# Preparing the first four attention units in another way: powers in PSUM, scaling on VectorE, the bonus by TensorE

## The chip, the cores and the metric

One core of one Trainium2 chip runs the whole kernel. The metric is the device time of one execution in microseconds; the number that stands for a kernel is the median of its runs.

## What is computed

Three stages follow each other. The first is a linear attention with a decaying state (4 sequences, 8 heads, 768 steps, head size 48), the other two are feed-forward networks over its 3072 output rows:

```
cur   = u * k_t (outer) v_t
y_t   = r_t . (state + cur)            # u is the bonus of the present step
state = w * state + k_t (outer) v_t    # w is the decay, one number per head and channel
h = max(x @ w1, x @ w2, x @ w3);  x = h @ w_out               # 384 -> 768 -> 384
g = x @ w_gate;  out = (silu(g) * (x @ w_val)) @ w_out2       # 384 -> 1536 -> 384
```

Everything is float32. A matmul of the networks is made of three at a faster type: each operand is split into a high part and a low part (`xhi`, `xlo` for inputs, two halves of `w_a`, `w_b`, `w_c` for weights), and the low times low product is left out.

## The kernel before

The 768 steps are six blocks of 128. With 4 sequences that makes 24 units; unit n is block n // 4, sequence n % 4. Blocks, not units, go through the networks: one block has 512 rows.

**A unit.** `load_unit` (L284) brings `qk` (r and k with channels down the partitions, 448 KB) and `nat` (k, v and r with time down the partitions, 576 KB). `prep_scores` (L299) multiplies r and k by a table `P` of powers of the decay, `scores` (L326) forms the 128x128 products per head in two PSUM banks. `prep_bonus` (L303) makes k * r * u on GpSimd, `bonus` (L312) sums it over a head's channels on VectorE into `a`, `fill` (L317) writes a diagonal matrix of it into `am` on ScalarE, eight instructions a unit, and `select` (L334) copies the scores below the diagonal over it on VectorE. `apply` (L341) multiplies `am` with v into the bank `y`; from unit 4 on it adds the state's part. `evacuate` (L364) copies `y` into the block's input `xr`. `prep_keys` (L308), `outer` (L371) and `update` (L389) keep the state.

**Weights.** They arrive in raw form and are rebuilt on the chip: a job k is half of a weight tile, fetched by SyncE (`fetch`), scaled on ScalarE (L225), put together by three VectorE instructions (L258, L259, L265), cast to the high half on ScalarE (`put_hi`, L270), and subtracted to give the low half (`put_lo`, L273, GpSimd or VectorE). There are three raw buffers, so fetch k waits for the last step of job k - 3.

**The first four units** (block 0) are prepared before any network work can begin. Before them VectorE builds `P` by doubling. When their rows are copied out, a branch follows (`branch`, L605): if a decay lies outside a range, a slow general loop recomputes everything. On these inputs it is not taken. Only after the branch are block 0's rows split into `xhi` (ScalarE, L410) and `xlo` (L414), and TensorE begins with m(0,0,0): the key m(i,f,j) is block i, output tile f of six, matrix j of three, nine matmuls of 128x512. Units 4 to 7 are prepared between block 0's groups, o(0,c) is the second product of the first network.

**The order** is written by a planner, `Plan` (L88). Each step names the engines that can do it with an estimated cost, and the steps it needs; TensorE's order is fixed by a list, and the others are filled in by estimated start times. Steps that share a read port between VectorE and GpSimd are listed in `SHARED`. Where the plan expects TensorE to stand still, `idle` inserts spare matmuls (`warm`). DMAs rotate over eight semaphores, so SyncE can issue a transfer only when the one eight places earlier has landed.

At the start SyncE also writes three blocks of zeros (768 KB each) to memory, `y_far` (L529): the inputs that the branch's general loop would have filled for blocks 3 to 5.

Of the kernel before, what the change touches and what calls it, by code (L numbers as in the profile page):

```python
# [88 lines left out]
class Plan:  # L89
# [9 lines left out]
    SHARED = ("top", "rest", "lo", "xlo", "ylo", "scaled", "bonus", "choose")  # L99
# [8 lines left out]
    def run(self, idle, hop=0.1):  # L108
# [32 lines left out]
        while ready:  # L141
# [4 lines left out]
            for k, options in ready.items():  # L146
                for e, t in options:
                    start, cost = max(t, free[e]), steps[k][0][e]
                    if e == "pool" or e == "dve" and k[0] in self.SHARED and (k[0], k[1] > 3) != ("scaled", True):
# [3 lines left out]
                    weight = rest[k] if k not in self.behind else rest[head] - self.behind[k]  # L153
                    rank = (start + shy - self.LOOK * weight, start + cost)
                    if best is None or rank < best[0]:
                        best = rank, k, e, start, cost
# [6 lines left out]
            if e == "pool" or e == "dve" and k[0] in self.SHARED and (k[0], k[1] > 3) != ("scaled", True):  # L163
# [10 lines left out]
def rwkv_moe(ctx: ExitStack, tc: tile.TileContext, qk, nat, kn, vn, rn, wcol, wh, uh, wup1, wout1, wup2, out):  # L174
# [106 lines left out]

    def load_unit(n):
        kvr = nat[n].rearrange("p (q h d) -> p q h d", q=3, h=H)
        if n in (2, 3):  # L284
            a = h_tile([112, 2, NPAIR, T], f"qk_{n}")
            c = h_tile([128, 2, H, D], f"kv_{n}")
            c = (c[:, 0], c[:, 1], r23[:, n - 2])
            nc.sync.dma_start(out=a, in_=qk[n].rearrange("p (q j t) -> p q j t", q=2, j=NPAIR))
            for x in range(3):
                nc.sync.dma_start(out=c[x], in_=kvr[:, x])  # L290
        else:
            a = atp.tile([112, 2, NPAIR, T], F32, tag="qk", name=f"qk_{n}")
            c = atp.tile([128, 3, H, D], F32, tag="nat", name=f"nat_{n}")
            nc.sync.dma_start(out=a, in_=qk[n].rearrange("p (q j t) -> p q j t", q=2, j=NPAIR))
            nc.sync.dma_start(out=c, in_=kvr)
            c = (c[:, 0], c[:, 1], c[:, 2])
        inp[n] = (a, c)

    def prep_scores(n, q, eng):  # L299
        a = inp[n][0][:, q]  # L300
        eng.tensor_tensor(out=a, in0=a, in1=late["P"] if n >= B else P[0:112], op=ALU.mult)
# [10 lines left out]
    def bonus(n):  # L312
# [590 lines left out]
```

## Time and profile before

| | us |
|---|---|
| runs | 860.22, 860.72, 862.56 (median 860.72) |
| profiled execution: its own time | 865.69 |
| profiled execution: span from first to last instruction | 864.0 |
| TensorE busy | 847.5 (98% of the span) |
| VectorE busy | 362.9 (42%) |
| ScalarE busy | 292.7 (34%) |
| GpSimd busy | 210.7 (24%) |
| mean granted TensorE clock | 0.993 |

Busy shares are averages over a start in which TensorE waits and a long rest in which it does not. In a timeline row, the idle time before an instruction and what ended it stand in brackets. A group's mean length mixes instructions that ran undisturbed with such that waited inside.

### The profile page before, as it was taken

To read this page: it belongs to the slowest core of one execution; us is meant where nothing else is said; L and a number is where in the kernel's file an instruction comes from. 1 tells how busy PE (TensorE), PEld (TensorE's weight loads), DVE (VectorE), ACT (ScalarE), POOL (GpSimd) and SP (SyncE) were. 2 spreads that over 40 slices of the span, in tenths; PEclk is the share of its full clock that TensorE was granted. 3 is DMA by queue.
4 is the path that set the end of the run, shared out by engine and by line. 5 is a ranking of instruction groups with operands and counts; after the bars stand their busy time and mean duration, and the time that the engine had idled before them with its cause. 6 is when DMAs were issued, how large, how long until landed. Compare 5 with 4: busy or idle time off the path is not lost.

```text
span 864.0 us, 11768 instructions
## 1 busy us (share of the span) xinstructions
PE 847.5 (98%) x4794; PEld 697.1 (81%) x4794; DVE 362.9 (42%) x545; ACT 292.7 (34%) x592; POOL 210.7 (24%) x188
## 2 busy tenths in 40 slices
PE   8889999999999999999999999999999999999998
PEld 7578678888888887888888888888888888888886
DVE  5578966627637735224377122222222222122221
ACT  5456553424434433213344221221122122113111
POOL 6756752514713702101224200010010010001000
PEclk9899999999999999999999999999999999999999
DMA  9567534445445632431132100010000000001001
GB/s 271 207 186 221 172 105 152 141 143 178 140 145 176 195 113 78 174 109 55 55 110 82 37 1 1 0 37 1 1 36 1 1 1 37 1 1 37 0 1 37
DMA packets 21720, 74.31 MB, mean 86 GB/s; under 512 B 2496, under 2 KB 3392, under 8 KB 20896
## 3 DMA queue, kind: packets, MB, share of 16 engines
q1 hardware_dynamic: 21664, 73.54, 26.2%
q8 instruction: 38, 0.62, 0.3%
q14 instruction: 18, 0.15, 0.1%
HBM read 58.39 MB, written 14.16 MB: 84 GB/s over the span
## 4 chain that ended last, share of the span: by engine, by line
PE 88%; DMA 3%; POOL 3%; DVE 2%; issue 2%; ACT 1%; SPq 1%; POOLq 0%; ACTq 0%; DVEq 0%
PE g L420 11%; PE g L421 11%; PE g L419 11%; PE m L419 8%; PE m L420 7%; PE m L421 7%; PE oo L420 6%; PE oo L421 6%; PE oo L419 6%; PE o L421 3%; PE o L419 3%; PE o L420 3%; PE s L332 2%; PE y L361 2%; PE y L352 2%
## 5 line engine op out<-in xcount | busy, mean ns | idle before, releaser
L419 PE MATMUL g<-xhi,w_c 128*128 128x512 f32 x432 | 168.0, 389 | 0.0
L420 PE MATMUL g<-xlo,w_c 128*128 128x512 f32 x432 | 168.0, 389 | 0.0
L421 PE MATMUL g<-xhi,w_c 128*128 128x512 f32 x432 | 168.0, 389 | 0.0
L476 DVE TENSOR_TENSOR g<-mm,g 128x512 f32<-128x512 f32 x72 | 50.1, 696 | 253.0 <-PE g L421 253.0
L419 PE MATMUL m<-xhi,w_a 128*128 128x512 f32 x324 | 129.9, 401 | 2.4 <-ACT h L433 2.3
L420 PE MATMUL m<-xlo,w_a 128*128 128x512 f32 x324 | 127.9, 395 | 3.1 <-POOL xlo L414 3.1
L421 PE MATMUL m<-xhi,w_a 128*128 128x512 f32 x324 | 126.9, 392 | 0.0
L414 POOL TENSOR_TENSOR xlo<-x,xhi 128x512 fp32r<-128x512 f32 x18 | 23.5, 1332 | 335.5 <-ACT xhi L410 335.5
L472 ACT ACTIVATE mm<-g 128x512 f32<-128x512 f32 x72 | 43.0, 597 | 156.8 <-PE g L421 156.8
L419 PEld LDWEIGHTS g<-xhi,w_c 128*128 128x128 f32 x432 | 81.1, 188 | 17.0
L421 PEld LDWEIGHTS g<-xhi,w_c 128*128 128x128 f32 x432 | 81.1, 188 | 16.8
L420 PEld LDWEIGHTS g<-xlo,w_c 128*128 128x128 f32 x432 | 81.1, 188 | 16.8
L481 ACT CAST gs<-g 128x512 fp32r<-128x512 f32 x72 | 42.3, 587 | 136.2 <-DVE g L476 136.2
L419 PE MATMUL oo<-gs,w_c 128*128 128x512 f32 x216 | 84.0, 389 | 0.0
L420 PE MATMUL oo<-gs,w_c 128*128 128x512 f32 x216 | 84.0, 389 | 0.0
L421 PE MATMUL oo<-gs,w_c 128*128 128x512 f32 x216 | 84.0, 389 | 0.0
L419 PEld LDWEIGHTS m<-xhi,w_a 128*128 128x128 f32 x324 | 61.2, 189 | 17.6 <-ACT h L433 2.4
L420 PEld LDWEIGHTS m<-xlo,w_a 128*128 128x128 f32 x324 | 61.2, 189 | 17.4 <-POOL xlo L414 5.6
L421 PEld LDWEIGHTS m<-xhi,w_a 128*128 128x128 f32 x324 | 61.3, 189 | 13.0
L453 DVE TENSOR_TENSOR gs<-g,gs 128x512 fp32r<-128x512 f32 x72 | 49.8, 692 | 46.6 <-ACT gs L481 46.6
L323 ACT ACTIVATE am<-aeye,a 128x128 f32<-128x128 f32 x192 | 59.6, 390 | 24.8 <-DVE a L315 24.7
L335 DVE COPY_PREDICATED am<-mask,s 128x512 f32<-128x512 uint8 x48 | 33.4, 735 | 45.5 <-PE s L332 40.1
(108 smaller groups left out, 1102.9 us busy)
## 6 DMA issues: line engine op xcount, KB each, us to landing
raw<-in_wup SPq DMA_DIRECT2D x36, 576.0 KB, 5.1
nat<-in_nat SPq DMA_DIRECT2D x22, 576.0 KB, 5.3
qk<-in_qk SPq DMA_DIRECT2D x24, 448.0 KB, 4.7
aside<-parts SPq DMA_DIRECT2D x12, 576.0 KB, 3.6
w_c<-aside SPq DMA_DIRECT2D x6, 1152.0 KB, 5.9
out<-ob SPq DMA_DIRECT2D x18, 256.0 KB, 2.1
y<-x SPq DMA_DIRECT2D x3, 768.0 KB, 9.6
raw<-in_wout SPq DMA_DIRECT2D x6, 384.0 KB, 3.7
```

The costliest lines, as they stand in the source:

```text
L323: eng.mul(o, aeye, f)
L332: nc.tensor.matmul(sc[n][x][:, j], a[r:r + D, 1, j], a[r:r + D, 0, j], start=True, stop=True)
L335: nc.vector.copy_predicated(ams[n][:, x], mask[:, None, :].to_broadcast([128, NPAIR, T]), sc[n][x])
L352: nc.tensor.matmul(y[r:r + m, j], st[b][r:r + D, j * D:j * D + m], a[r:r + D, 0, j], start=j == 0, stop=False, skip_group_check=True)
L414: eng.tensor_tensor(out=lo[:, k], in0=t[:, k], in1=hi[:, k].bitcast(F32), op=ALU.subtract)
L419: nc.tensor.matmul(p, wh_, xh, start=first, stop=False)
L420: nc.tensor.matmul(p, wh_, xl, start=False, stop=False)
L421: nc.tensor.matmul(p, wl_, xh, start=False, stop=last)
L453: nc.vector.tensor_tensor(out=g[1], in0=p, in1=g[0].bitcast(F32), op=ALU.subtract)
L472: nc.scalar.activation(out=hs[i, f], in_=banks["g", i, f, 0], func=AF.Silu)
L476: nc.vector.tensor_tensor(out=p, in0=hs[i, f], in1=p, op=ALU.mult)
L481: nc.scalar.copy(t[:, 0], banks["g", i, f, 1])
```

## The change

- `P` is copied once into a PSUM bank, `powers`, before the first unit; `prep_scores` reads it there and always runs on VectorE (before: VectorE or GpSimd, table in SBUF, for units 0 to 3).
- For units 0 to 3 the bonus comes from TensorE: `product_columns` multiplies the channel layout of r (read backwards) with k, one instruction (VectorE for unit 0, GpSimd for 1 to 3), and `diagonal` multiplies four 112-row tiles of it with `uE`, the bonus weights as two columns a tile. r in time layout is not loaded for these units, and `prep_bonus` and the sum on VectorE fall away. `uE` comes from a small load, a transpose and two copies.
- `fill` of the odd heads of units 1 to 3 is one GpSimd instruction in place of four on ScalarE.
- Loads are cut and moved: columns and v of the four units first, then three raw weights, then the four k, then `u`; columns of units 4 and 5 and the fourth raw weight are issued ahead of the branch.
- Block 0's rows are not gathered in `xr`: `upper` writes `xhi` and `lower` writes `xlo` straight from each `y` bank, ahead of the branch. `prep_keys` of the four units comes after the branch, and their outer products after m(0,f,2).
- The zeros of `y_far` are written inside a second branch, `plain_far`, after m(1,1,0).
- The planner picks each step's engine by end time first, and its starting times and costs are new. With that, some low halves of weights in block 0 move from GpSimd to VectorE.

```diff
+    def product_columns(n, eng):
+        a = inp[n][0]
+        eng.tensor_tensor(out=prods[0:112, n % 2], in0=a[:, 0, :, ::-1], in1=a[:, 1], op=ALU.mult)
+    def diagonal(n):
+        for j in range(NPAIR):
+            nc.tensor.matmul(diag[:, 2 * j:2 * j + 2], prods[0:112, n % 2, j], uE[0:112, j], start=True, stop=True)
...
+        if n < B:
+            (eng.copy if eng is nc.scalar else eng.tensor_copy)(a0s[n], diag[:, 0:H])
+        else:
+            nc.vector.tensor_reduce(out=a0s[n], in_=inp[n][1][2], axis=AX.X, op=ALU.add)
...
+    def upper(n):
+        nc.scalar.copy(next(halves(n)), ys[n][:, 0:NK])
+    def lower(n):
+        hi, lo = halves(n)
+        nc.vector.tensor_tensor(out=lo, in0=ys.pop(n)[:, 0:NK], in1=hi.bitcast(F32), op=ALU.subtract)
...
-        for y in y_far:
-            nc.sync.dma_start(out=y, in_=x2[1])
...
+        nc.scalar.copy(powers, P[0:112])
...
+        def plain_far(_):
+            with tc.If(late["general"] == 0):
+                for y in y_far:
+                    nc.sync.dma_start(out=y, in_=x2[FAR - 1])
...
-        order = [(q, n) for q, n in zip("ssyyssyy", (0, 1, 0, 1, 2, 3, 2, 3))]
+        order = [("d", 0), ("s", 0), ("d", 1), ("s", 1), ("d", 2), ("y", 0), ("s", 2), ("d", 3), ("y", 1),
+                 ("s", 3), ("p", 0), ("y", 2), ("y", 3)]
...
-                add(("fetch", k), {"sync": 0.5}, [("rest", k - 3), ("branch",)] + pace, lambda e, k=k: fetch(k), lag=3.5, **own)
+                add(("fetch", k), {"sync": 0.5}, [("rest", k - 3)] + pace, lambda e, k=k: fetch(k), lag=3.5, **own)
...
-            for k in range(NK):
+            for k in range(NK if i else 0):
                 add(("xhi", i, k), {"act": 0.63}, there, lambda e, i=i, k=k: split_hi((1, i), xr[i], k))
```

VectorE ahead of the branch, before, from unit 0's scaling on (`qk` columns, `a` bonus sums, `am` the matrix that `select` completes, `s` scores):

```order
L301 TENSOR_TENSOR qk_108<-qk_108,P 112x512 x2
L315 TENSOR_REDUCE a_0_227<-nat_109 128x8
L335 COPY_PREDICATED am_228<-mask,s_0_216 128x512
L335 COPY_PREDICATED am_228<-mask,s_0_217 128x512
L315 TENSOR_REDUCE a_1_267<-nat_114 128x8
...
L335 COPY_PREDICATED am_268<-mask,s_1_249 128x512
L315 TENSOR_REDUCE a_2_302<-r_106 128x8
L335 COPY_PREDICATED am_268<-mask,s_1_250 128x512
```

The same stretch of VectorE now:

```order
L316 TENSOR_TENSOR prods<-qk_113 112x512
L312 TENSOR_TENSOR qk_113<-qk_113,powers 112x512 x2
L362 COPY_PREDICATED am_221<-mask,s_0_230 128x512
L312 TENSOR_TENSOR qk_117<-qk_117,powers 112x512
L362 COPY_PREDICATED am_221<-mask,s_0_231 128x512
L312 TENSOR_TENSOR qk_117<-qk_117,powers 112x512
L312 TENSOR_TENSOR qk_121<-qk_121,powers 112x512 x2
L362 COPY_PREDICATED am_253<-mask,s_1_272 128x512
L362 COPY_PREDICATED am_253<-mask,s_1_273 128x512
L312 TENSOR_TENSOR qk_125<-qk_125,powers 112x512 x2
L408 TENSOR_TENSOR xlo_212<-y_290,xhi_211 128x3x128
```

The sums are gone; all eight scalings, and the low part of the first unit's rows, stand between the selects.

SyncE's queue at the start, before, from unit 1 on (`raw` weights, `y` the zeros):

```order
L294 DMA qk_113<-in_qk 112x1024
L295 DMA nat_114<-in_nat 128x1152
L288 DMA qk_117<-in_qk 112x1024
L290 DMA kv_118<-in_nat 128x384 x2
L290 DMA r_106<-in_nat 128x384
L288 DMA qk_123<-in_qk 112x1024
L290 DMA kv_124<-in_nat 128x384 x2
L290 DMA r_106<-in_nat 128x384
L216 DMA raw_129<-in_wup 128x1152
```

And now, from unit 0 on, up to the columns of units 4 and 5 and the fourth raw weight:

```order
L290 DMA qk_113<-in_qk 112x1024
L298 DMA nat_115<-in_nat 128x384
...
L290 DMA qk_125<-in_qk 112x1024
L298 DMA kv_127<-in_nat 128x384
L218 DMA raw_129<-in_wup 128x1152
...
L308 DMA nat_115<-in_nat 128x384
...
L290 DMA qk_349<-in_qk 112x1024
L290 DMA qk_374<-in_qk 112x1024
L218 DMA raw_404<-in_wup 128x1152
```

The last unit's columns are the seventh transfer counted from unit 0's columns, before they were the tenth; the keys come after the first weights.

VectorE just after the branch now (`w_a` and L275: the low half of a weight):

```order
L260 TENSOR_SCALAR t_426<-t_426 128x576
L261 SCALAR_TENSOR_TENSOR t_426<-raw_133,t_426 128x576
L275 TENSOR_TENSOR w_a_402<-t_347,w_a_402 128x576
L267 SCALAR_TENSOR_TENSOR t_426<-raw_133,t_426 128x576
L312 TENSOR_TENSOR qk_349<-qk_349,powers 112x512 x2
L480 TENSOR_TENSOR h_0_647<-h_0_647,m_0_1_633 128x512
```

Before, no low half stood on VectorE here; now five of `w_a`, one of `w_b` and two of block 1's three `xlo` do.

## Rows read from the trace of the kernel before

**Rows 1.** The chain that ended last, 5 to 38 us: start, us, what.

```profile
5.74 11.07 DMA r<-in_nat
...
20.15 3.72 POOL qk L301 x3
```

**Rows 2.** Busy time by stretch: PE, PEld, DVE, ACT, POOL, PEclk, DMA share, GB/s.

```profile
58.00:98.10 40.10, 39.98 (x355) 32.89 (x354) 36.97 (x57) 24.83 (x56) 25.97 (x22) 1.00 0.67 205
...
36.20:105.65 69.45, 64.05 (x511) 50.89 (x510) 58.66 (x84) 39.71 (x87) 45.39 (x36) 0.98 0.64 196
...
110.20:864.00 753.80, 749.81 (x4003) 618.69 (x4002) 283.54 (x415) 231.40 (x452) 136.46 (x115) 1.00 0.21 68
```

**Rows 3.** Timeline of TensorE, 36 to 110 us: start, us, instruction, [idle before].

```profile
36.20 0.49 PE L419 MATMUL m<-xhi,w_a 128*128 128x512 f32 x1
...
40.91 1.13 PE L380 MATMUL u<-nat 128*64 128x48 f32 x32
...
53.42 0.53 PE L419 MATMUL m<-xhi,w_a 128*128 128x512 f32 x1 [2.25 <-ACT h L433]
...
54.17 0.63 PE L421 MATMUL m<-xhi,w_a 128*128 128x512 f32 x1
54.60 0.63 PE L419 MATMUL m<-xhi,w_a 128*128 128x512 f32 x1
...
61.38 1.08 PE L352 MATMUL y<-qk,st 48*64 48x128 f32 x16
...
64.95 0.50 PE L419 MATMUL m<-xhi,w_a 128*128 128x512 f32 x1
...
98.11 0.39 PE L419 MATMUL o<-hs,w_b 128*128 128x512 f32 x1
98.34 0.39 PE L420 MATMUL o<-hs,w_b 128*128 128x512 f32 x1
...
109.81 0.40 PE L421 MATMUL m<-xhi,w_a 128*128 128x512 f32 x1
```

**Rows 4.** Groups of VectorE instructions, 36.2 to 110 us: busy, mean ns, idle before.

```profile
L265 DVE SCALAR_TENSOR_TENSOR t<-raw,t 128x576 uint16<-128x576 uint32 x10 | 11.6, 1155 | 0.2
L259 DVE SCALAR_TENSOR_TENSOR t<-raw,t 128x576 uint32<-128x576 uint32 x10 | 9.2, 924 | 0.3
L301 DVE TENSOR_TENSOR qk<-qk,powers 112x512 f32<-112x512 f32 x12 | 7.8, 680 | 3.8 <-DMA qk<-in_qk 3.8
L335 DVE COPY_PREDICATED am<-mask,s 128x512 f32<-128x512 uint8 x8 | 5.8, 743 | 1.1 <-ACT am L323 1.1
L258 DVE TENSOR_SCALAR t<-t 128x576 uint32<-128x576 uint32 x10 | 5.0, 496 | 3.8 <-ACT t L225 3.6
...
L453 DVE TENSOR_TENSOR hs<-m,hs 128x512 fp32r<-128x512 f32 x3 | 2.1, 687 | 0.0
```

**Rows 5.** Timeline of VectorE ahead of the branch.

```profile
5.74 2.86 DVE L301 TENSOR_TENSOR qk<-qk,P 112x512 f32<-112x512 f32 x2 [0.21 <-DMA qk<-in_qk]
...
30.97 0.80 DVE L265 SCALAR_TENSOR_TENSOR t<-raw,t 128x576 uint16<-128x576 uint32 x1
...
32.94 1.90 DVE L265 SCALAR_TENSOR_TENSOR t<-raw,t 128x576 uint16<-128x576 uint32 x1
```

**Rows 6.** Timeline of ScalarE at the branch.

```profile
35.53 1.66 ACT L410 CAST xhi<-xr 128x512 fp32r<-128x512 f32 x3 [0.64 <-DVEq L608]
```

**Rows 7.** Busy time by stretch, the first 20 us; columns as in rows 2.

```profile
0.00:10.00 10.00, 7.94 (x56) 7.63 (x57) 6.01 (x23) 4.61 (x4) 5.49 (x18) 1.00 0.73 210
10.00:20.00 10.00, 9.31 (x94) 8.13 (x93) 4.62 (x10) 5.61 (x19) 7.49 (x7) 1.00 1.05 309
```

**Rows 8.** Groups of GpSimd instructions, 36.2 to 110 us.

```profile
L273 POOL TENSOR_TENSOR w_a<-t,w_a 128x576 fp32r<-128x576 f32 x11 | 17.0, 1547 | 16.1 <-ACT w_a L270 16.1
L414 POOL TENSOR_TENSOR xlo<-xr,xhi 128x512 fp32r<-128x512 f32 x6 | 7.7, 1326 | 2.0 <-ACT xhi L410 2.0
...
L310 POOL TENSOR_TENSOR nat<-nat,PT 128x384 f32<-128x384 f32 x5 | 5.8, 1157 | 0.0
```

More of the change, by code (lines that the diff above doesn't have):

```diff
@@ L280, in h_tile, with natural @@
         return moe1.tile(shape, dt, tag="h", name=name, bufs=NF1)
-    def load_unit(n):
[L283 to L297, printed above, removed]
+    def natural(n):
+        return nat[n].rearrange("p (q h d) -> p q h d", q=3, h=H)
@@ L642, in rwkv_moe @@
             new = []
-            if q == "s" and n in (1, 3):
-                new = [("select", n, 0), ("select", n, 1)]
+            if key in (("y", 1), ("y", 3)):
+                new = [("low", n)]
             elif q == "u" and n < (NB - 1) * B:
@@ L722, in rwkv_moe @@
             for q in range(2):
[L723 removed]
+                add(("scaled", n, q), {"dve": 0.69}, [("prod", n) if first else ("load", n)],
                     lambda e, n=n, q=q: prep_scores(n, q, engine[e]))
[L725 to L727 removed]
@@ L728, in rwkv_moe @@
-            pair = {2: 0, 4: 2}.get(n, n - 1 if n > 4 else None)
-            add(("s", n), {"pe": 1.3}, [("scaled", n, 0), ("scaled", n, 1)] + bank_free["s", n]
-                + ([("select", pair, 0), ("select", pair, 1)] if pair is not None else []), lambda e, n=n: scores(n))
-            add(("a0", n), {"dve": 0.55}, [("bonus", n)] + ([("y", two)] if n > 1 else []), lambda e, n=n: bonus(n))
+            add(("keys", n), {"pool": 0.97}, [("keyed", n), ("low", B - 1)] if first else [("bonus", n)], lambda e, n=n: prep_keys(n))
@@ L732, in rwkv_moe @@
+            pair = n - 1 if n else None
+            add(("s", n), {"pe": 1.3}, [("scaled", n, 0), ("scaled", n, 1)]
+                + ([("select", pair, x) for x in range(2)] if pair is not None else []),
+                lambda e, n=n: scores(n))
+            add(("a0", n), {"dve": 0.2, "act": 0.25} if first else {"dve": 0.55}, [("d" if first else "bonus", n)] + ([("y", two)] if two is not None else []),
+                lambda e, n=n: bonus(n, engine[e]))
             for x in range(2):
-                add(("fill", n, x), {"act": 1.6}, [("a0", n)],
+                add(("fill", n, x), {"pool": 1.35} if 0 < n < B and x else {"act": 1.6}, [("a0", n)],
@@ L740, in rwkv_moe @@
-            add(("u", n), {"pe": 0.02 if last else 0.6}, [("y", n), ("keys", n)] + ([("branch",)] if first else []) + bank_free["u", n]
-                , lambda e, n=n: outer(n))
+            add(("y", n), {"pe": 1.75 if first else 2.15}, [("select", n, 0), ("select", n, 1)]
+                + {0: [], 2: [("turned",)], 4: [("low", 2)]}.get(n, bank_free["y", n] if first else [("row", n - 1)]) + ([] if first else [("update", n - B)]), lambda e, n=n: apply(n))
+            if first:
+                add(("row", n), {"act": 0.55}, [("y", n)], lambda e, n=n: upper(n))
+                add(("low", n), {"dve": 0.58}, [("row", n)], lambda e, n=n: lower(n))
+            else:
+                add(("row", n), {"act": 0.6}, [("y", n)] + ([("xlo", i - 1, k) for k in range(NK)] if i > 1 else []),
+                    lambda e, n=n: evacuate(n))
@@ L742, in rwkv_moe @@
+            add(("u", n), {"pe": 0.02 if last else 0.6}, [("y", n), ("keys", n)] + ([("branch",)] if first else []) + bank_free["u", n], lambda e, n=n: outer(n))
             if first:
```

186 lines of the change are left out of this document (116 added, 70 removed).

## The prediction

> **What bounds the kernel now.** I read the busy time by stretch first. From 110.2 us on TensorE is busy for 749.81 of 753.80 us [rows 2]: nothing can be won there, and the change leaves its matmuls as they are. So only the time until TensorE gets there counts. I mark that place by the end of block 1's first group, m(1,0,0): its last matmul runs from 109.81 to 110.21 [rows 3]. Whatever brings this end forward by x us brings the end of the kernel forward by x, as long as nothing later runs dry.
>
> Two parts lie ahead of the mark. The first ends with the first network matmul at 36.20 us [rows 3]. The chain of waits shows what sets it: a load of r that lands at 16.81, 11.07 us after it could be issued, then GpSimd, which does unit 2's and unit 3's bonus and scaling one behind the other, 3.72 us for three scalings [rows 1]. VectorE is no limit there: 6.01 and 4.62 us busy in the first two tens [rows 7]. The second part, 36.20 to 110.21, takes 74.0 us. The least TensorE needs for it comes from its timeline: 18 groups of block 0, three groups of the second product and m(1,0,0), 22 x 9 = 198 matmuls 0.227 us apart (98.34 - 98.11, finer over many), 45.0 us; four passes over a unit (state, `am` times v, outer product, next scores) at 64.95 - 61.38 = 3.57 us, 14.3; and two pairs of early outer products at 1.07, 2.1 [rows 3]. That is 61.4 us, so 12.6 us are lost. Some lie at the start and the end, where each low part comes from GpSimd at 1.33 us [rows 8], some at 53.42, where TensorE had stood for 2.25 us and then ran its matmuls 0.43 us apart (54.17, 54.60) instead of 0.23 [rows 3], which is the 1.2 GHz level of its clock after a pause. From 58 to 98 it loses nothing, but VectorE is then busy for 36.97 of 40.10 us [rows 2]: it is the next limit.
>
> **The front, up to the first network matmul.** Removed: r's loads for four units (4 x 192 KB), GpSimd's bonus and scaling, four sums on VectorE. Added on VectorE: one product and all eight scalings. The scaling of unit 0 with the table in SBUF took 2.86 us for two while GpSimd worked [rows 5]; the same instruction with the table in PSUM takes 0.68 on average, GpSimd working or not [rows 4]. So 9 x 0.68 = 6.1 (the product is not shown in the trace; it is of the same shape; below, the same 0.68, above 1.43, half of the 2.86). Eight selects at 0.743 [rows 4] are 5.9. Four low parts from `y`, 128x384: not shown; by the 128x512 subtraction at 0.687 [rows 4] three quarters, 0.52, at most 0.69: 2.1. Two weight jobs stand in this stretch before and after: 0.496 + 0.924 + 1.155 = 2.58 each [rows 4], 5.2, collisions with GpSimd included. Sum 19.3 us, in one queue.
>
> It starts at 5.74, when the first columns land [rows 5]; they are the first big load in both orders. Is anything later than VectorE? Unit 3's columns and v end 4 x 640 KB = 2.62 MB into the stream; at 210 GB/s for 10 us and 309 after [rows 7] that is 11.7 us, and VectorE gets to them at about 14. The first raw weight ends at 3.2 MB, 13.6 us, and is wanted near 18. GpSimd has eight steps of a tile each (three products, three fills, one table, one low half), 10.6 us at 1.33 [rows 8], in 20; ScalarE gives it 12 of its 32 fills and gets small copies for them. TensorE's new transposes and small matmuls (four of 2 columns a unit) lie between scores that wait for VectorE anyway; they are covered, and without that cover cost at most one pass over a unit, 3.57. One wait stays: the first select needs unit 0's scores, and only one more scaling can fill it, 1.2 us. Then the branch: 0.64 us from VectorE's passing to the next ScalarE step [rows 6]. 5.74 + 19.3 + 1.2 + 0.64 = 26.9. The first matmul comes 9.3 us earlier, and its low parts are already there. Bounds: 25 (no collisions, no wait) and 30 (the product at 1.43, three more collisions of 1.90 - 0.80 = 1.1 [rows 5], TensorE's small matmuls on the path).
>
> **Block 0, from there to the mark.** TensorE alone would be at the mark at 26.9 + 61.4 = 88.3. VectorE has more. Before, it was busy for 58.66 us between the first matmul and m(1,0,0) [rows 2]. To that come five low halves of `w_a` at 0.687 x 576/512 = 0.77, one of `w_b` at 0.52 and two `xlo` at 0.687, together 5.7. GpSimd loses those and the three `xlo` of block 0 (5 x 1.33, 5 x 1.55, about 1.2) and gains four keys at 1.16 [rows 8]: from 45.4 to about 34 us [rows 2]. The collisions that stretch L265 from 0.80 [rows 5] to 1.155 [rows 4] should shrink by a quarter: -1. Sum 63.4. Idle VectorE before: 69.45 - 58.66 = 10.8 [rows 2], of which 3.8 ended with late columns and 3.8 with a late first weight step [rows 4]; both loads are now issued ahead of the branch, so 3.2 stays. 26.9 + 63.4 + 3.2 = 93.5, and behind the last `xlo` two matmuls, 0.7: **94.2**. The gain is 110.2 - 94.2 = 16.0 us: 9.3 from the front, 6.7 from the stalls behind it.
>
> What else moves costs nothing by the rows. The three writes of zeros go from 17 us into block 1, where DMA runs at a fifth of its time [rows 2]; SyncE has unit 10's loads ahead of them. Keys and outer products of units 0 to 3 come later; the state that they make is needed by unit 4's pass, two groups on. The second branch is priced by the first one: between 0 and 0.64 [rows 6], I take 0, since TensorE's queue is full there. The Trainium skill (Runtime: NRT & Kernel Launch, Instruction fetch mechanics) says that a taken branch to code outside the fetched pages stalls until a transfer has brought it; by that rule the sum would be up to 0.64 worse, and no row here shows such a fetch.
>
> **The sum.** The profiled execution took 865.69 with a span of 864.0, so its own time would become 849.7. It lies 5 us above the median of the runs; the change acts on the same stages in each, so from the median 860.72 - 16.0 = **844.7**.
>
> **Rivals.**
> - TensorE sets the pace of block 0, VectorE hides in it: the mark comes at 88.3, gain 21.9, **838.8**. For it: VectorE's 58.66 contain waits inside instructions that fewer GpSimd steps would shorten. Against: 63.4 of VectorE work do not fit into 61.4.
> - The port: the moved low halves, all operands in SBUF, collide. A collision costs 1.1 us (1.90 against 0.80 [rows 5]); if all eight moved steps meet one, 8.8 us, gain 7.2, **853.5**. For it: 2.86 for two scalings beside GpSimd [rows 5]. Against: GpSimd works a quarter less. The Trainium skill (SBUF — State Buffer, Who interferes with whom) states it as a lock: a VectorE step with two SBUF inputs and a GpSimd step that reads SBUF wait for each other's whole length. By that rule each moved step could wait up to a full GpSimd step. Rows 5 agree with it; what they do not tell is how often the two meet.
> - The front comes late: loads or GpSimd's products hold the queue. First matmul at 31, mark at 98.3, gain 11.9, **848.8**. For it: the load that waited 11.07 us [rows 1] was late although issued early. Against: up to the last columns 2368 KB come in, before 3712.
> - Slower: the clock. If VectorE makes TensorE pause often in block 0, its matmuls run 0.43 instead of 0.23 apart as at 54.17 [rows 3]. Over the 189 matmuls from the first group through the second product this is 37.8 us, against the 16.0: **882.5**. It decides from 80 slow matmuls on. For it: one pause of 2.25 us had that effect. Against: it lasted some ten matmuls, and the forecast's pauses are spread.
> - The change does not do what it says: VectorE's idle 10.8 stay, since raw weights come no faster; gain 8.4, **852.3**.
>
> **How the numbers follow.** About 0.3% (2.6 us) is what a measurement of this kernel can tell from no change. Forecast 0.50 (its own range 841 to 847), TensorE-bound 0.18, front late 0.16, port 0.07, idle stays 0.05, clock 0.04. All but the clock are faster by more than 0.3%; of the port and idle cases I give 0.02 to mixtures that end near no change. The range 838.5 to 851.0 takes in the first three; outside lie port, idle, clock and an edge of the TensorE case, some 0.2. Faster 0.94, same 0.02, slower 0.04.
>
> **What would show it.** First network matmul near 26.9; VectorE nearly gapless from 5.7 to 26 and again to 93; no wait for r or for columns in the chain; m(1,0,0) ending near 94; 753.8 us behind it as before. The forecast is wrong if VectorE has idle stretches of microseconds in block 0 while TensorE waits too (then a load or ScalarE sets the pace), if L275 averages near 1.9, if the clock row shows long half-rate stretches, or if TensorE waits after the mark, at the second branch or for unit 11's loads behind the zeros.

## The result and the profile after

The changed kernel takes **854.36 us** (median of four runs, 853.85 to 855.24), the kernel before 861.64 in the runs beside it: ratio 0.9917, 95% interval 0.9897 to 0.9937. It is faster, by 7.3 us; the forecast was 844.7 with a range of 838.5 to 851.0, so it missed by 9.7 us and the range does not hold the time.

In the profiled execution (own time 855.24, span 853.3) the mark, the end of m(1,0,0), stands at 99.64 us. Timeline of TensorE at the first network matmul and at the mark, after the change:

```profile
10.65 2.48 PE L619 MATMUL spare<-tmp 128*128 128x128 f32 x20
...
27.91 0.50 PE L461 MATMUL m<-xhi,w_a 128*128 128x512 f32 x1
...
99.24 0.40 PE L463 MATMUL m<-xhi,w_a 128*128 128x512 f32 x1
```

They answer to the first and the last row of [rows 3]: the first network matmul came at 36.20 and comes at 27.91, the mark went from 110.21 to 99.64. Busy time by stretch, from the first network matmul up to the end of block 1's last `xlo` (VectorE's last step ahead of the mark), and behind the mark (columns as in [rows 2]):

```profile
27.90:98.90 71.00, 65.33 (x517) 50.55 (x516) 67.27 (x94) 37.67 (x84) 39.37 (x33) 1.00 0.57 180
99.65:853.30 753.65, 749.76 (x4002) 618.81 (x4002) 305.36 (x455) 232.86 (x459) 83.13 (x74) 1.00 0.21 71
```

Behind the mark lie 753.65 us where there were 753.80 [rows 2]: nothing was won or lost there, as forecast. Between first network matmul and mark, the stretch called block 0 below, lie 71.7 us (99.64 - 27.91) where 67.3 were forecast (94.2 - 26.9). VectorE is busy for 67.27 of 71.00 us there, so it is the likely limit, but with more work than the sum had. Groups of VectorE instructions from 27.9 to 98.9:

```profile
L261 DVE SCALAR_TENSOR_TENSOR t<-raw,t 128x576 uint32<-128x576 uint32 x10 | 12.9, 1288 | 0.3
L267 DVE SCALAR_TENSOR_TENSOR t<-raw,t 128x576 uint16<-128x576 uint32 x10 | 8.9, 895 | 0.1
L312 DVE TENSOR_TENSOR qk<-qk,powers 112x512 f32<-112x512 f32 x11 | 7.1, 678 | 0.3 <-DMA qk<-in_qk 0.3
L260 DVE TENSOR_SCALAR t<-t 128x576 uint32<-128x576 uint32 x10 | 6.8, 677 | 0.3 <-DVEq L666 0.3
...
L275 DVE TENSOR_TENSOR w_a<-t,w_a 128x576 fp32r<-128x576 f32 x5 | 4.4, 881 | 0.5 <-ACT w_a L272 0.3
...
L456 DVE TENSOR_TENSOR xlo<-xr,xhi 128x512 fp32r<-128x512 f32 x2 | 2.7, 1367 | 0.0
L444 DVE COPY_PREDICATED xr<-slow,x 128x1536 f32<-128x1536 uint8 x1 | 2.6, 2611 | 0.3 <-DMA xr<-xr 0.3
L267 DVE SCALAR_TENSOR_TENSOR t<-raw,t 128x384 uint16<-128x384 uint32 x3 | 2.5, 830 | 0.1
...
L261 DVE SCALAR_TENSOR_TENSOR t<-raw,t 128x384 uint32<-128x384 uint32 x3 | 1.7, 559 | 0.1
```

Against [rows 4], L267 (there L265) fell from 1155 to 895 ns, but L261 (L259) rose from 924 to 1288 and L260 (L258) from 496 to 677; the moved steps take 881 and 1367 ns, where 0.77 and 0.687 us were forecast. The scalings, whose table lies in PSUM, kept their 680 ns (now 678). How a weight gets late shows in the timeline of four engines around 62 us:

```profile
59.34 0.67 ACT L272 CAST w_a<-t 128x576 fp32r<-128x576 f32 x1 [2.81 <-DVE t L267]
...
61.16 1.02 POOL L329 TENSOR_TENSOR nat<-nat,PT 128x384 f32<-128x384 f32 x1
...
62.13 1.63 POOL L275 TENSOR_TENSOR w_a<-t,w_a 128x576 fp32r<-128x576 f32 x1
...
62.53 1.84 DVE L261 SCALAR_TENSOR_TENSOR t<-raw,t 128x576 uint32<-128x576 uint32 x1
...
63.81 0.51 PE L463 MATMUL m<-xhi,w_a 128*128 128x512 f32 x1 [1.26 <-POOL w_a L275]
```

VectorE's L261, 0.76 us in other places of the same trace, takes 1.84 beside GpSimd's low half; GpSimd's takes 1.63; and TensorE stands for 1.26 us until that low half is there. The meeting is only part of the lateness: the high half was there at 60.01, and GpSimd came to the low half at 62.13, behind its steps for a unit's bonus and keys.

### The profile page after: what moved, and what is told of

The parts are those of the page before. It is cut to its first block, busy times and chain, and to the rows that moved or that the text cites. A ratio compares the mean times of both kernels' runs of the same rounds, so it can differ in the third digit from the quotient of the medians.

```text
span 853.3 us, 11757 instructions
## 1 busy us (share of the span) xinstructions
PE 841.5 (99%) x4791; PEld 692.7 (81%) x4791; DVE 394.7 (46%) x601; ACT 288.1 (34%) x583; POOL 136.9 (16%) x130
## 4 chain that ended last, share of the span: by engine, by line
PE 93%; DVE 2%; DMA 1%; POOL 1%; issue 1%; ACT 1%; SPq 0%; POOLq 0%; ACTq 0%; DVEq 0%
PE g L463 11%; PE g L462 11%; PE g L461 11%; PE m L461 8%; PE m L463 8%; PE m L462 8%; PE oo L463 6%; PE oo L461 6%; PE oo L462 6%; PE s L359 3%; PE o L462 3%; PE o L461 3%; PE o L463 3%; PE y L389 2%; PE y L380 2%; PE spare L619 1%
## 5 line engine op out<-in xcount | busy, mean ns | idle before, releaser
L463 PEld LDWEIGHTS m<-xhi,w_a 128*128 128x128 f32 x324 | 60.8, 188 | 17.8 <-POOL w_a L275 3.5
L351 ACT ACTIVATE am<-aeye,a 128x128 f32<-128x128 f32 x180 | 55.8, 391 | 17.4 <-DVE a L341 17.2
L492 ACT CAST hs<-m 128x512 fp32r<-128x512 f32 x33 | 19.4, 586 | 89.1 <-DVE m L480 88.7
```

Of the source, the lines that this page charges most:

```text
L351: eng.mul(o, aeye, f)
L463: nc.tensor.matmul(p, wl_, xh, start=False, stop=last)
L492: nc.scalar.copy(hsplit[i, f][0], banks["m", i, f, 2])
```

## The experiments

Two theories were tried after the result, one for each of two steps of the sum. **A**: the profiled execution of the kernel before was itself late ahead of the mark, so a gain measured against it must not be taken off the median. **P**: in block 0 GpSimd's steps stretch VectorE's, so each step put on either engine there costs more than its own length. Rivals: profiling adds a fixed time (B, against A); the chain of a weight job through four engines sets the pace whatever VectorE's load (L, against P). What the profiled executions showed, in us, the mark read as above ("between" is block 0):

| kernel (label) | own time | first network matmul | mark | between | behind |
|---|---|---|---|---|---|
| before, on record | 865.69 | 36.20 | 110.2 | 74.0 | 753.8 |
| before (b_again1) | 860.25 | 33.10 | 104.8 | 71.7 | 753.7 |
| before (b_again2) | 865.30 | 36.80 | 109.8 | 73.0 | 753.8 |
| changed, result | 855.24 | 27.91 | 99.6 | 71.7 | 753.7 |
| changed (a_again) | 861.30 | 34.61 | 105.7 | 71.1 | 753.6 |
| a_nospare | 855.88 | 27.85 | 100.3 | 72.4 | 753.6 |
| a_lopool | 853.98 | 27.88 | 98.6 | 70.7 | 753.7 |
| a_fetchbranch | 854.23 | 28.00 | 98.5 | 70.5 | 753.7 |
| a_nokeys | 856.10 | 34.59 | 100.5 | 65.9 | 753.7 |
| a_zerosearly | 856.52 | 27.90 | 101.1 | 73.2 | 753.6 |
| f_turn | 854.42 | 27.64 | 98.8 | 71.1 | 753.6 |
| f_turn_lo | 857.84 | 34.34 | 102.5 | 68.2 | 753.6 |
| f_turn_act | 852.67 | 27.42 | 97.0 | 69.6 | 753.6 |
| f_turn_lo_act | 859.26 | 34.74 | 103.9 | 69.2 | 753.7 |
| f_dense | 851.32 | 28.27 | 96.0 | 67.7 | 753.6 |

**1. Both kernels once more, unchanged.**

> The kernel before, once more, unchanged. Theory A: its profiled execution on record (865.69 us, 4 us above the median of its runs now known, 861.6) carried lateness of its own ahead of the mark, which a typical execution lacks: loads that landed late (the raw weights at 42.8 to 51.7 us) and the half-rate matmuls behind that at 53.4 us. By A a new profile that takes about 861 us has its mark (end of block 1's first group) near 106 us instead of 110.2, with about 753.8 us behind it, and the gap at 53 us is gone or smaller. Rival B: the mark stands at 110 again and the distance between profiled execution and runs is a fixed cost of profiling, so that the 10.6 us between the two traces are the true gain of the stages.

> The same kernel a second time, to see how far the mark moves between executions. Theory A: its first network matmul and its mark differ from the first look's by some us (36.2 and 110.2 on record), always with the same 753.8 us behind the mark, so own time follows the mark one to one. Rival B: within 0.5 us of each other.

> The changed kernel, once more, unchanged. Theory A (lateness belongs to the kernel before, whose loads sat closest to their use): first network matmul 27.9 and mark 99.6 again within 1 us, own time 854 to 855.5. Rival: the changed kernel's mark moves as much as that of the kernel before, 2 us or more.

The kernel before took 860.25 and 865.30 us. First network matmul in the execution of 860.25, and the stretch behind its mark:

```profile
33.10 0.50 PE L419 MATMUL m<-xhi,w_a 128*128 128x512 f32 x1
```

```profile
104.80:858.50 753.70, 749.78 (x4002) 618.67 (x4002) 283.81 (x415) 231.23 (x452) 136.39 (x115) 1.00 0.20 68
```

A holds, B falls: own time follows the mark one to one. In that execution block 0 took 71.7 us, which is what the changed kernel takes, and the first network matmul came 3.1 us earlier than in the one on record; the load of r in its chain of waits landed at 14.92 us there, at 16.81 in the one on record [rows 1]. The rival of the third expectation holds too: the changed kernel's second execution (a_again) took 861.30. Loads don't explain it: VectorE began its scalings at 7.26 us in both. TensorE's pace does. Timeline of TensorE in that execution:

```profile
5.50 2.93 PE L619 MATMUL spare<-tmp 128*128 128x128 f32 x12
...
15.08 4.61 PE L619 MATMUL spare<-tmp 128*128 128x128 f32 x20
...
34.61 0.50 PE L461 MATMUL m<-xhi,w_a 128*128 128x512 f32 x1
```

The twenty passes that took 2.48 us in the result's trace take 4.61: about half pace until some 19.7 us, though the granted clock is given as 1.00 for the same stretch. First that stretch in a_again and VectorE's first select there, then the stretch in the result's trace:

```profile
6.00:20.00 14.00, 14.00 (x74) 13.33 (x74) 5.67 (x9) 5.27 (x18) 5.80 (x5) 1.00 1.05 332
```

```profile
13.55 0.73 DVE L362 COPY_PREDICATED am<-mask,s 128x512 f32<-128x512 uint8 x1 [5.01 <-PE s L359]
```

```profile
6.00:20.00 14.00, 14.00 (x161) 12.80 (x161) 10.58 (x19) 9.46 (x30) 7.67 (x7) 1.00 1.05 336
```

TensorE is busy for all of these 14 us in both, but gets through 74 records instead of 161, and VectorE waits 5.01 us for unit 0's scores where it had waited 1.39. So TensorE's queue of spares and small matmuls is the limit of the front at half pace: 6.7 us later at the first network matmul.

**2. No spare matmuls at the branch.**

```
-            warm(8)
             general = late["general"] = nc.values_load(...)
```

> The changed kernel without the eight spare matmuls ahead of the first branch. In its trace TensorE is in them from 25.88 to 27.93 and the first network matmul starts at 27.91, while VectorE's last low part ends at 27.19. Theory: they hold the first matmul by about 0.5 us, so without them it comes at about 27.4, the mark at 99.1, and the time falls by 0.5 us at most. Rival: TensorE, idle for about 1.5 us, falls to the lower clock for its first matmuls, as the kernel before did behind its pause at 53 us (0.43 instead of 0.23 us apart), and the time rises by 1 to 4 us.

856.06 us (ratio 0.9926, 0.9899 to 0.9953), 1.7 above the changed kernel, though the intervals overlap; the mark is 0.7 later. The theory falls, and the trace shows what the rival said. Timeline of TensorE, and the granted clock by stretch:

```profile
27.85 0.50 PE L461 MATMUL m<-xhi,w_a 128*128 128x512 f32 x1 [1.95 <-ACTq L665]
...
29.80 0.63 PE L461 MATMUL m<-xhi,w_a 128*128 128x512 f32 x1
...
32.31 0.40 PE L461 MATMUL m<-xhi,w_a 128*128 128x512 f32 x1
```

```profile
28.00:32.00 4.00, 4.00 (x12) 3.08 (x13) 3.94 (x5) 1.46 (x3) 0.76 (x1) 0.60 0.52 154
```

The first matmul does not come earlier, since it waits for ScalarE's passing of the branch; and after standing for 1.95 us TensorE runs some eight matmuls 0.43 apart, the 1.2 GHz level as at 54.17 in [rows 3].

**3. One part undone: low halves, fetches, zeros.** Three kernels. First, all low halves of block 0's weights on GpSimd again:

```
-add(("lo", k), {"pool": 1.2 * share, "dve": 0.76 * share}, ...
+add(("lo", k), {"pool": 1.2 * share} if k < nearly else {"pool": ..., "dve": ...}, ...
```

> The changed kernel with all low halves of block 0's weights on GpSimd, as in the kernel before: VectorE loses five steps of 0.88 us and one of 0.55 ahead of the mark. Theory V (VectorE's queue sets the pace of block 0: 67.3 us busy of 71.0, and TensorE's 7 us of waits there are for weights that VectorE unpacks late): block 0 falls from 71.7 to 67 to 69 us and the time by 2 to 4 us. Rival P (the two engines share a port): the six steps come back as longer VectorE steps beside GpSimd, L267 goes from 0.90 back to the 1.16 of the kernel before, VectorE's busy time falls by less than 2 us, block 0 stays within 1 us of 71.7 and the time within 1 us. Rival S: the low half on GpSimd takes 1.3 to 1.6 us instead of 0.9 and each weight is later, slower by 1 to 2 us.

853.63 us (0.9895, 0.9869 to 0.9921), block 0 70.7 us: 1.0 less than in the result (0.4 less than in a_again), close to what P said. Busy time, and two groups of VectorE:

```profile
27.88:97.90 70.02, 65.19 (x517) 50.59 (x517) 64.70 (x88) 37.65 (x83) 48.63 (x36) 1.00 0.56 182
```

```profile
L261 DVE SCALAR_TENSOR_TENSOR t<-raw,t 128x576 uint32<-128x576 uint32 x10 | 11.7, 1166 | 0.3
L267 DVE SCALAR_TENSOR_TENSOR t<-raw,t 128x576 uint16<-128x576 uint32 x10 | 11.1, 1112 | 0.2
```

VectorE lost steps of 5.0 us (5 x 0.881 + 0.547) and its busy time fell by 2.6 (by 1.3 against a_again's 66.02); L267 went from 895 back to 1112 ns. So moving the low halves to VectorE bought nothing.

Second, the fetches behind the branch again:

```
-add(("fetch", k), {"sync": 0.5}, [("rest", k - 3)] + pace, ...
+add(("fetch", k), {"sync": 0.5}, [("rest", k - 3), ("branch",)] + pace, ...
```

> The changed kernel with the raw weights from the fourth on held behind the first branch again, as in the kernel before. By the prediction's term for the late first weight step (VectorE idle 3.6 us before L258 waiting for ScalarE's t, 2.3 in the execution of 860.25) block 0 becomes longer by 2.3 to 3.6 us. Rival: VectorE has other work queued there and the wait is filled, less than 0.7 us.

Block 0 took 70.5 us, not longer: the rival holds, an early fetch is worth nothing here. The runs lay in two groups, 853.7 to 856.3 and 860.3 to 861.6 (four of ten), as far apart as half pace made them above; the median of 855.73 (0.9946, 0.9921 to 0.9972) says only how many of each there were.

Third, the zeros at the start and no second branch:

```
+for y in y_far:
+    nc.sync.dma_start(out=y, in_=x2[1])
...
-            with tc.If(late["general"] == 0): ...
```

> The changed kernel with the three writes of zeros back at the start (issued behind the first loads) and without the second branch. The prediction put the move at 0: then block 0 stays at 71 to 71.7 and the time at 854.4, or 861 at half pace. Rival D (2.36 MB of writes in the stretch where raw weights and columns come in): loads land later, VectorE waits for columns again (3.8 us in the kernel before), first matmul or block 0 1 to 4 us later.

855.83 us (0.993, 0.9916 to 0.9945), each of its four runs between 855.2 and 856.5, block 0 73.2: rival D, in its lower part. By the medians and by the mark (101.1 against 99.6) the move of the zeros is worth some 1.5 us, which the prediction put at 0; the intervals of the two ratios overlap, so the size is not clear of noise. The second branch, also gone here, lies behind the mark, where 753.6 us show no cost of it. VectorE waits 0.8 us for columns in block 0 there, 0.3 in the changed kernel. TensorE waits 1.81 us for a weight at 65 us, in the changed kernel 1.26, and falls to half rate behind that; granted clock from 64 to 68:

```profile
64.00:68.00 4.00, 2.73 (x8) 2.16 (x9) 4.00 (x6) 2.55 (x8) 2.19 (x2) 0.73 0.88 258
```

**4. GpSimd's bonus and key steps of units 0 to 9 left out.** Their results are missing from the output.

```
 def prep_bonus(n, eng):            def prep_keys(n):
+    if n < 10: return              +    if n < 10: return
```

> The changed kernel with GpSimd's bonus products and key scalings of units 0 to 9 left out (so those of units 0 to 9 are missing from the output); all else stays in its order. GpSimd loses some 20 of its 39 us between the first network matmul and the mark, VectorE loses no step. Theory P (the weight steps L260, L261 and L267 on VectorE are stretched by steps of GpSimd that run at the same time, and this sets the length of block 0): L261 falls from 1.29 us towards 0.76 and L267 from 0.90 towards 0.80, VectorE's busy time by 4 to 8 us, TensorE's 7 us of waits for weights shrink to below 3 and block 0 goes from 71.7 to 66 to 68 us. Rival L (two weight jobs in flight, each passing ScalarE, VectorE, ScalarE and one of two engines, set the pace whatever VectorE's load): VectorE's idle time grows by what its steps lose, and block 0 stays at 70 to 71.5.

One execution: block 0 took 65.9 us, 5.8 less than in the result and 5.2 less than in a_again, whose front also ran at half pace. Busy time, and three groups of VectorE:

```profile
34.60:99.80 65.20, 63.84 (x517) 50.80 (x517) 59.83 (x95) 37.63 (x84) 15.01 (x13) 1.00 0.61 196
```

```profile
L261 DVE SCALAR_TENSOR_TENSOR t<-raw,t 128x576 uint32<-128x576 uint32 x10 | 9.1, 907 | 0.3
L267 DVE SCALAR_TENSOR_TENSOR t<-raw,t 128x576 uint16<-128x576 uint32 x10 | 8.2, 823 | 0.1
...
L260 DVE TENSOR_SCALAR t<-t 128x576 uint32<-128x576 uint32 x10 | 6.3, 626 | 0.3 <-DVEq L670 0.3
```

P holds, L falls. GpSimd lost 24.4 us (39.37 to 15.01), and VectorE, which lost no step, 7.4 us of busy time (67.27 to 59.83): 0.30 us for each us of GpSimd beside it, or 0.25 against a_again (66.02 and 39.66). The block follows: it is VectorE's busy time and 4.4 to 6.1 us more in this kernel, in a_lopool and in the changed one. The Trainium skill (SBUF — State Buffer, Who interferes with whom) says that a VectorE step with two SBUF inputs and a GpSimd step that reads SBUF exclude each other. The rows of L261 and L267, which read two tensors from SBUF, agree, and so do the scalings that read `powers` in PSUM and did not change; L260, which reads one, fell only from 677 to 626. What this test leaves mixed is GpSimd's own queue: without those steps its low halves also come sooner, and TensorE's waits for GpSimd's low halves of `w_a`, 2.2 us in the changed kernel, are gone. That this queue alone sets the block is not borne out, since a_lopool puts more steps into the queue (48.63 us) and its block is not longer; no run separates the two.

**5. What moves out of block 0 without leaving work out.** The power table for the keys made and turned early, and the keys of units 0 and 1 ahead of the branch (f_turn); with the low halves on GpSimd (f_turn_lo); with the state's decay on ScalarE for units 4 to 7 instead (f_turn_act); all three (f_turn_lo_act):

```
-order = [("d", 0), ("s", 0), ("d", 1), ... ("s", 3), ("p", 0), ("y", 2), ("y", 3)]
+order = [("d", 0), ("s", 0), ("p", 0), ("d", 1), ... ("s", 3), ("y", 2), ("y", 3)]
-add(("p2",), {"pool": 1.07, "dve": 0.65}, [("prod", B - 1)], ...
+add(("p2",), {"pool": 1.07}, [], ..., at=5.7)
-add(("keys", n), {"pool": 0.97}, [("keyed", n), ("low", B - 1)] if first else ...
+add(("keys", n), {"pool": 0.97}, [("keyed", n)] if first else ...
...
-add(("decay", n), {"pool": 0.54}, ...
+add(("decay", n), {"act": 1.0} if n < 2 * B else {"pool": 0.54}, ...
```

> The changed kernel with the power table for the keys made by GpSimd at 5.7 us, turned by TensorE behind unit 0's scores (before: behind unit 3's, where y of unit 2 waits for ScalarE's copy of it from 21.5 to 22.7), and the keys of units 0 and 1 scaled ahead of the branch where GpSimd is idle (20.2 to 24.5 us). Theory: the front ends 0.6 to 1.1 us earlier (first network matmul 26.8 to 27.3), and block 0 is 0.3 to 1 us shorter since two steps of GpSimd of 1.4 us no longer run beside VectorE's weight steps there; time 0.9 to 2 us less than the changed kernel. Rival: the keys collide with VectorE's weight steps ahead of the branch instead (L260, L261 and L267 of the first two weights), the front is no shorter, and the gain is below 0.5 us.

> The same with block 0's low halves on GpSimd, which alone made block 0 about 0.7 us shorter. Theory: the two add, another 0.5 to 1 us. Rival: GpSimd, which also has keys ahead of the branch, is late with the first low halves, and it is 0 to 1 us slower than without.

> The first kernel with the decay of the state of units 4 to 7 on ScalarE (four small steps each) in place of GpSimd's four steps of 0.8 us. By the price that leaving out some 20 us of GpSimd's work showed (block 0 shorter by 5 to 5.8 us, about 0.25 us for each us of GpSimd) this is worth 0.8 us in block 0. Rival: ScalarE's queue, with 16 more small steps, is late with casts that TensorE waits for: 0 to 1 us slower.

> All three together. Theory: the gains add, 2 to 3 us less than the changed kernel's 854.4. Rival: one of the two additions costs, and the best of the other three stays ahead.

f_turn came out in two groups, four runs of 853.6 to 854.7 and five of 860.3 to 861.5; its trace shows 27.64 and 71.1, so front and block gained 0.3 and 0.6 us, but its four faster runs lie where the changed kernel's four do (853.9 to 855.2): nearer the rival. **f_turn_lo is the fastest: 851.38 us** (0.9878, 0.9863 to 0.9894), four runs from 851.0 to 852.8 and one of 857.8 at half pace, the profiled one. Block 0 in it took 68.2 us with VectorE busy for 62.33:

```profile
34.34:101.80 67.46, 64.33 (x516) 50.80 (x517) 62.33 (x88) 38.25 (x84) 46.94 (x34) 1.00 0.58 189
```

Against a_lopool, which has the same low halves on GpSimd, GpSimd is busy for 1.7 us less (46.94 for 48.63) and VectorE, with the same steps, for 2.4 less (62.33 for 64.70): with two keys out of the way the steps of the two probably meet less often, which no row shows directly. f_turn_act took 852.88 (0.9894, 0.9878 to 0.9911), with block 0 at 69.6 where f_turn had 71.1, so alone the decay on ScalarE gained 1.5 us of block 0 in this trace, 0.8 being expected. f_turn_lo_act took 858.82 (0.9932, 0.9903 to 0.9961), four of seven runs from 858.8 to 860.6 and the others 852.2 to 854.6, with block 0 at 69.2 where f_turn_lo had 68.2: the decay on ScalarE adds nothing to the low halves, as its rival said.

**6. The half-pace front.** First, without the planner's 15 spares (`warm(max(0, ...))` replaced by `pass`), and with u's load issued by SyncE:

> The changed kernel without the 15 spare matmuls that its planner puts into TensorE's gaps between the units' steps (3, 10 and 2); those ahead of them and at the branch stay. In one execution of the changed kernel (861.3 us) TensorE ran the front at half pace until 19.7 us (20 passes in 4.61 us instead of 2.48) and the first network matmul came at 34.6 instead of 27.9. Theory C (at half pace TensorE's queue is the limit of the front, and spares in it only add): where it is at full pace nothing changes (27.9), and where it is at half pace the first matmul comes 3 to 6 us earlier than 34.6. Rival: without them TensorE is idle for longer and stays at half pace in every execution, first matmul 30 to 34 and the time 2 to 6 us longer than the changed kernel's 854.4.

> The changed kernel with the small load of u issued by SyncE right behind the load of w, not by ScalarE. In the changed kernel it lands at 5.35 us, TensorE stands for 0.66 us before it, ScalarE starts its table load only at 2.37 and gives VectorE the powers at 7.22 (VectorE waits 0.79 for them). Theory: the load lands near 3 us, the powers near 6.1, VectorE's 0.79 goes and the first network matmul comes 0.4 to 1 us earlier, time 0.4 to 1 us less. Rival: SyncE issues the first columns 0.45 us later, and TensorE's pace at the front, which rises from half to full near 5.5 us, decides: no difference or, at half pace, 5 us more.

Without those spares the runs were 857.1 to 859.8 (four) and 863.0 to 866.3 (six), median 863.20 (0.9992, 0.9963 to 1.002), and the first network matmul of its trace, at half pace, came at 39.18, later than a_again's 34.61. Theory C falls: both groups lie above those of the changed kernel, so the spares shorten the front. Its rival, half pace in every execution, does not fit two groups either; the lower one was not profiled. f_un gave 854.68 (0.9913, 0.9886 to 0.9940), first matmul 28.19: no gain, its rival. Then the front with the wait filled by spares, alone (f_front) and with the low halves on GpSimd (f_both), and with the first spares in one unbroken run, alone (a_dense) and in f_turn_lo (f_dense):

```
-warm(7)
+warm(11)
 nc.tensor.matmul(diag[:, H:], ones, off[:, 0:NPAIR], ...)
 nc.tensor.transpose(turned_u, un, ...)
...
-warm(6)
+warm(2)
```

> The changed kernel with the load of u issued by SyncE behind that of w, four of the six spare matmuls put ahead of the small transpose that waits for it, and the powers copied before ScalarE's two small copies. In the two executions at half pace TensorE had stood for 0.29 and 0.16 us just before that transpose; where the same kernels ran at full pace the gap was there too (0.66 and 0.32). Theory G (an unbroken run of spares past 6 us lets TensorE's pace rise near 5.5 us every time): all runs within 2 us of 854, none near 861, first network matmul 27.2 to 27.9. Rival H (which of the two it is doesn't hang on the gap): one run in three to six stays near 861 as in the kernel whose fetches wait for the branch (4 of 10).

> The same front with all low halves of block 0's weights on GpSimd. That step alone made block 0 70.7 us long instead of 71.7 and the median 853.6. Theory: the two add, 852.5 to 853.5. Rival: the front gains nothing, 853.6, or half-pace fronts near 860 turn up in its runs too.

> The changed kernel with eleven spare matmuls in one run at the start (from 1.44 us to about 6), then the two small matmuls that had cut that run at 4.6 us, then two spares more; the powers are copied before ScalarE's two small copies, the flag's sum on VectorE moves behind unit 1's scores. Theory G: with no cut in the first run the pace rises every time; no run above 857, median 854.4 or up to 0.5 lower. Rival H: the pace at the front falls one way or the other regardless, and 1 to 3 of the runs are near 861.

> The same front in the kernel with the power table made early, two keys ahead of the branch and block 0's low halves on GpSimd, whose runs were 851.0 to 852.8 and once 857.8. Theory G: all runs within 1.5 us of 851.4 and none near 858, so faster than the kernel before by 1.2% and than the changed one by 3 us. Rival H: a run or more near 858; or the small copies, now 1 us later, delay unit 0's selects and the whole is 0.5 to 1 us slower.

f_front gave 855.54 (0.9928, 0.9915 to 0.9940), none of its five runs near 861, but the first matmul at 28.97, since TensorE waits 0.53 and 0.72 us for the products of units 0 and 1, whose columns were issued later. f_both gave 854.29 (0.9925, 0.9899 to 0.9950), one of six runs at 860.7, so filling the wait does not keep the group away: there rival H holds. a_dense gave 854.73 (0.9920, 0.9901 to 0.9939) and f_dense 852.18 (0.9898, 0.9875 to 0.9921). None of their twelve runs is in a group 5 to 7 us above the others; one of f_dense, 855.8, lies some 4 us above, with a mean granted clock of 0.994 where its others have 0.999 or 1.0, so not all are within the 1.5 us that G gave it. In the changed kernel and the nine that keep its first spares and its load of u (a_nospare, a_lopool, a_fetchbranch, a_nokeys, a_zerosearly and the four f_turn kernels), 16 of 53 runs lay in such a group. Four of those 16 were profiled, and all four show half pace. First spares of f_dense, and its first network matmul:

```profile
1.44 5.06 PE L619 MATMUL spare<-tmp 128*128 128x128 f32 x22 [1.44 <-POOL tmp masks.py:199]
...
28.27 0.50 PE L461 MATMUL m<-xhi,w_a 128*128 128x512 f32 x1 [0.56 <-ACTq L665]
```

G holds for the one unbroken piece, so far as twelve runs can tell. The kernel before points the same way: its first spares are one piece too, and in its three profiled executions the 16 passes of unit 0's scores took 1.16 us each time, in a_again 2.08. The unbroken piece costs 0.4 to 0.6 us at the first matmul (28.27 against 27.64, 28.35 against 27.91). f_turn_lo has the lowest median, f_dense is the kernel without a group near 858; their intervals overlap.

## Why the prediction was wrong

Of the 9.7 us two steps account for 9.4, the baseline and block 0; a third, the front, was off by 1.0.

**From the profiled execution to the median: 5.0 us.** The step is "the change acts on the same stages in each, so from the median 860.72 - 16.0". The stages that the change acts on are those that made the profiled execution 5 us longer than the median: in it VectorE waited 3.8 us for columns and 3.6 for the first weight step [rows 4], in the execution of 860.25 us 1.1 and 2.3, with block 0 at 71.7 instead of 74.0, and the first network matmul came 3.1 later. The change takes that lateness away, and a shorter execution has less of it to lose. The predicted mark was an absolute one; 94.2 with 753.8 behind it and 1.7 of difference between span and own time is 849.7, as the text had it, and that, not 844.7, is what its sum gave. Against the execution of 860.25 the changed kernel's gain of about 5 us lies wholly in the front (33.10 to 27.91); block 0 takes 71.7 us in both, so nothing was won there, where the forecast had 6.7.

**Block 0: 4.4 us (71.7 for 67.3).** That VectorE limits it is borne out by experiment 4 (67.27 of 71.00 busy), and its idle time (3.7 for 3.2) and the tail (0.7) were near. The term "Sum 63.4" was 3.9 too small (2.6 in a_again, with 66.02). The moved steps were priced without GpSimd beside them: 5 x 0.881 + 0.547 + 2 x 1.367 = 7.7, not 5.7. And the collisions that "should shrink by a quarter: -1" did not. Before, beside [rows 4], the smaller forms and the choice of block 1's input took:

```profile
L265 DVE SCALAR_TENSOR_TENSOR t<-raw,t 128x384 uint16<-128x384 uint32 x3 | 3.2, 1061 | 0.1
L259 DVE SCALAR_TENSOR_TENSOR t<-raw,t 128x384 uint32<-128x384 uint32 x3 | 2.8, 947 | 0.1
...
L405 DVE COPY_PREDICATED xr<-slow,x 128x1536 f32<-128x1536 uint8 x1 | 1.9, 1908 | 0.0
```

With their smaller forms, L267 gave back 3.4 us and L261 took 2.6 more; L260 took 1.8 more and the choice of the input 0.7. Together with the moved steps that is 4.7 where 3.9 are missing, since the records of a group overlap a little and busy time counts such overlaps once. One premise failed with it: GpSimd was to fall from 45.4 to about 34 us, and was busy for 39.37, because its steps were stretched too (the bonus L325 takes 1512 ns, before, as L306, 1094), one more unit's fell into the stretch, and the text took off five `xlo` from a row whose stretch [rows 2] holds four. The port rival named the mechanism and priced it at 853.5, close to the time, but for another sum: it had collisions only on the moved steps.

**The front: 1.0 us (27.9 for 26.9).** VectorE's work was overestimated: from 5.77 to the end of its last low part at 27.19 lie 21.4 us with 3.7 of waits, so 17.8 of work instead of 19.3. The waits were underestimated, 3.7 instead of 1.2: 2.4 for scores, 0.8 for the powers' copy, 0.5 for a high part. TensorE's small matmuls, which the text called covered, lie at least in part on the path: the chain that ended last runs from 5 to 28 us through TensorE's queue nearly throughout, with spares between. The spares at its end cost nothing, for a_nospare's first matmul came at 27.85 without them; the turning of the keys' table (`pt_ps`, then ScalarE's `PT`) cost about 0.3, which f_turn got back by doing it early (27.64).

```profile
10.79 2.34 PE spare L619 x20
13.12 1.09 PE s L359 x16
14.22 0.98 PE diag L320 x8
...
21.54 0.60 PE pt_ps L639 x4
...
22.17 0.49 ACT PT L642
...
25.95 1.98 PE spare L619 x16
27.93 0.48 PE m L461
```

Against these stands -0.9: the profiled execution of the result lies 0.9 above its median, and its own time is 1.9 above its span instead of 1.7. 5.0 + 4.4 + 1.0 - 0.9 + 0.2 = 9.7.

**Smaller points.** The zeros' move, put at 0, came out at about 1.5 us, not clear of noise; that it is because they then run outside the stretch where weights and columns come in is argued. The early fetch, to which part of the 6.7 us was given, is worth nothing. The second branch and the later outer products show no cost, and the 753.8 us were right. The clock rival did not come about in block 0, whose granted clock is 1.00 (0.98 in a_again), but half pace in the front, which no rival named, costs 6.7 us in some executions of the changed kernel.

**Left open.** What makes the front of one execution run at half pace and not another's was not settled beyond the runs above. Neither was it separated how much of block 0 is VectorE's stretched steps and how much is low halves waiting in GpSimd's queue. More buffers for weights in flight were not tried.

## What to carry to other kernels

A gain is the difference of two whole times of the same kind: where the stages that are to shrink vary between executions, work out the new absolute time, or profile the kernel before several times first, and do not take a gain read from one long execution off the median. An engine's sum must price each moved step by its row beside the neighbour that it shares a port with, and each step of that neighbour as a cost to the engine (here 0.25 to 0.30 us for 1 us of GpSimd), even if it is "off the path". A test that leaves the neighbour's work out shows what it costs in all, though not by which of its ways.

## What was not expected of the hardware

TensorE ran spares at about half pace up to 19.7 us while the granted clock was given as 1.00. By their times 16 of 53 runs with the changed kernel's first spares did so, and none of twelve when eleven spares came in one piece from 1.44 us. The Trainium skill (TensorE: Matmul & The Clock Gate, What's actually happening) says that the number of slow matmuls at the start differs from run to run and puts the cost below 1% of a kernel. Here it is 6.7 of 855 us, which agrees, and is nearly as much as the change gained; that it is the same slowness is not shown, since the granted clock gives no sign of it.

Which of two steps is stretched when VectorE and GpSimd meet was not fixed here. The choice of block 1's input, one `copy_predicated` of 128x1536, took 1.91 us in a_nokeys, where GpSimd stood idle. In the result's trace it began 0.15 us behind a GpSimd step and took 2.61:

```profile
91.02 1.00 POOL L324 TENSOR_TENSOR nat<-nat 128x384 f32<-128x384 f32 x1
...
91.17 2.61 DVE L444 COPY_PREDICATED xr<-slow,x 128x1536 f32<-128x1536 uint8 x1 [0.31 <-DMA xr<-xr]
```

In the kernel before it took 1.91 beside a GpSimd step, and that step, the decay of a state, took 2.52 where those of the changed kernel take 0.92 on average:

```profile
101.09 2.52 POOL L387 TENSOR_TENSOR st<-st,pw 112x192 f32<-112x192 f32 x1
...
101.38 1.91 DVE L405 COPY_PREDICATED xr<-slow,x 128x1536 f32<-128x1536 uint8 x1
```
